# An attention and token/channel mixer kernel on one core: two key transposes and some sixty other steps change their places in a hand-written order

## The chip, the cores and the metric

The kernel runs on one NeuronCore of a Trainium2 chip. Its engines each work through a queue of their own, in order: TensorE (PE in the profile; its weight loads are PEld), VectorE (DVE), ScalarE (ACT), GpSimd (POOL) and SyncE (SP), which here only issues DMAs. The metric is the device time of one execution in microseconds.

## The reference

Eight batches, eight heads, 576 positions, head dimension 64. Keys and values are averaged over groups of eight positions (72 keys a head); the attention output of all heads forms x (576 x 512), which goes through a token mixer (576 to 256 to 576, with a residual) and a channel mixer (512 to 1536 to 512, with a residual).

```python
k_p = k.reshape(B, H, Sp, pool, D).mean(axis=3)
v_p = v.reshape(B, H, Sp, pool, D).mean(axis=3)
scores = scale * np.matmul(q, k_p.transpose(0, 1, 3, 2))
attn = softmax(scores)
x = np.matmul(attn, v_p)                        # heads side by side: (B, 576, 512)
h = np.maximum(xt @ w_tok1, 0.0) @ w_tok2       # xt: x with its two last axes exchanged
u = x + h.transpose(0, 2, 1)
out = u + np.maximum(u @ w_ch1, 0.0) @ w_ch2
```

## The kernel before

The work is cut into nine units (unit, L868). Units 0 to 7 run the channel mixer of 512 of the 576 rows of batch n; unit 8 runs the rows that are left of all batches. Between its matmuls, unit n carries the attention and token mixer of the next batches, so that TensorE always has something to do. The main work of a unit is a generator (unit_fast, L694) that yields 48 times, and after yield i the steps that PLAN[n] (L22) lists under i are issued: this is a *slot*. In units 0 to 5, slots 0 to 23 lie between halves of the twelve l1_tile (L557: four 512-column matmuls each, L560, then a ScalarE activation into GT, L564). The eight products that follow have twelve 256-column matmuls each (L699), yield after every four, and end with VectorE sums (L739, s and o). They form the second channel matmul with seven multiplications of blocks instead of eight, and so need sums of GT and of the weights, made by VectorE: "=1" (L603), "=2", "=3", "=4" (L588). In units 6 to 8 the first channel matmul is done in the same manner; the string under -1 in PLAN orders its steps (A1 to C7, L675), with L for a half tile and X for a third of the first product, and y0 to y3 and z0 to z3 make the sums that it needs (Y: on GpSimd).

A step "b.name" belongs to batch b. Those that matter here:

- lk, lq, lv: DMAs that load a batch's keys, queries, values, issued by GpSimd.
- K0, K1 (k0, V0, V1, v1 likewise): the average over eight positions of one half of the heads by three additions (pool8, L214: lines 217, 218 and 221 for keys, 223 for values), on GpSimd for capital letters and on VectorE for small ones. Both halves of the keys write the tile kp.
- kpT (L262): four TensorE transposes (L265) of kp and a ScalarE copy into kD. It needs both halves.
- Q0, Q1: VectorE transposes of the queries (L321). s0, s1, s2 (L326): scores, with the exponentials on ScalarE (L343); they need kD.
- av0 to av4 (L414): attention times values, then reciprocal and multiplication on VectorE (L426, L365) or, for aw, on ScalarE (L369).
- at0, at1 (L430): the first token matmul, five 512-column matmuls (L434) and a ScalarE activation into AT. u0 to u4 (L441): the second, and the residual on VectorE (L457).
- t0 to t3: transposes of u by TensorE (L465). Later batches do it by a write of u to HBM and a read in another shape (M0, M2, M4 and M, MT, on SP's queue), and a VectorE transpose of 32x32 blocks (T0 to T5, L499).
- g (gate, L864): VectorE sets a flag and GpSimd copies it (L866). What stands behind the copy on GpSimd therefore waits until VectorE has come so far; and VectorE's next setting of the flag waits until GpSimd has made the copy before.

Most TensorE steps write one of four PSUM banks, p1a to p1d. take (L82) hands out the bank that was given back first; a step that takes a bank waits on the chip until the engine that read it last is done. Scores and av steps use two other buffers ("p").

Of the kernel before, what the change touches and what calls it, by code (L numbers as in the profile page):

```python
# [20 lines left out]
HEAD = """LkA LkT LkB LvT Lq LvA LvB Lt1 Lk1 Lt2 Lc1b Lc1a Lq1 Lc1c Lv1 Lc1d p1 Lc2a Lc2b Lc2c d2 d2 d3 d1 d4 d4 c0 c1 prep q0 kp0 kp1 kt0 q1 d1 o0 kt1 kp2 e0 e1 q3 kt2 o1 q2 e3 vpool0 o3 e2 a00 vpool1 a02 o2 m01 d1 d1 m00 a04 X1 m03 a14 m02 X0 m04 p0 a10 a12 1.kpool m10 m14 m12 m13 m11 A1 A0 X2 X3 A2 A3"""  # L21
PLAN = [  # L22
# [9 lines left out]
]  # L32


# [906 lines left out]
```

## Time and profile before

| what | us |
|---|---|
| time, median of 3 runs | 260.82 (260.37 to 261.18) |
| the profiled execution, whole | 261.66 |
| its span, first to last instruction | 259.9 |
| TensorE busy in the span | 253.5 |
| VectorE / GpSimd / ScalarE busy | 206.7 / 149.5 / 128.7 |

The granted TensorE clock is 0.999 of full speed over the span. In a timeline row stand the start, the duration, engine, line, operation, the tiles (output<-inputs), shapes, and how many equal instructions the row merges; in brackets the engine's idle time before it and what ended it. TensorE's durations overlap, so that a matmul's price is read from the distance between starts.

### The profile page before, as it was taken

How to read it: one execution, taken by the hardware profiler on the slowest of the kernel's cores; microseconds unless marked ns; L12 is line 12 of the kernel's file. 1: busy time of each engine (PE TensorE's matmuls, PEld its weight loads, DVE VectorE, ACT ScalarE, POOL GpSimd, SP SyncE). 2: the span in 40 equal slices, each digit the busy share in tenths (PEclk: the TensorE clock that was granted, in tenths of full speed). 3: DMA queues.
4: the chain of work that ended last, by engine and by line, in shares of the span. 5: the costliest groups of instructions: out<-in, count | busy, mean ns of one | idle time of the engine just before them, and what ended most of it. 6: DMA issues, size and time to landing. Idle time of an engine off the chain costs nothing.

```text
span 259.9 us, 5596 instructions
## 1 busy us (share of the span) xinstructions
PE 253.5 (98%) x2211; PEld 169.3 (65%) x2211; DVE 206.7 (80%) x413; ACT 128.7 (50%) x242; POOL 149.5 (58%) x161
## 2 busy tenths in 40 slices
PE   8999999999989999999999999999999999999994
PEld 2785466764656644774478447844686678888883
DVE  5557569997768755898799586987999699999994
ACT  3354875049727565547652576056516631622720
POOL 8656226899989999678969983886211001411000
PEclk9999999999999999999999999999999999999999
DMA  7999999993074798569933883660225051702304
GB/s 142 194 201 206 205 207 209 206 230 91 3 117 65 120 226 160 167 102 226 247 93 53 192 215 83 91 162 2 103 62 156 9 159 45 203 3 49 115 3 161
DMA packets 31931, 34.32 MB, mean 132 GB/s; under 512 B 2976, under 2 KB 23968, under 8 KB 31904
## 3 DMA queue, kind: packets, MB, share of 16 engines
q0 software_dynamic: 17856, 17.64, 43.1%
q1 hardware_dynamic: 13632, 15.93, 20.1%
q10 hardware_dynamic: 416, 0.39, 0.5%
q8 instruction: 17, 0.28, 0.4%
q14 instruction: 10, 0.08, 0.1%
HBM read 38.99 MB, written 12.58 MB: 198 GB/s over the span
## 4 chain that ended last, share of the span: by engine, by line
PE 77%; DMA 13%; DVE 4%; POOL 2%; issue 2%; DVEq 0%; POOLq 0%
PE p1b L699 9%; PE p1c L699 8%; DMA w_ch<-in_moe_w_ch_dram 7%; PE p1c L560 6%; PE p1a L560 5%; PE p1d L560 5%; PE p1a L699 5%; PE p1b L560 5%; PE p1d L699 5%; DMA area<-in_moe_w_tok_dram 4%; PE p L334 3%; PE p L422 3%; DMA kr<-in_k_dram 3%; PE p1d L675 3%; PE p L675 2%; PE p1b L434 2%
## 5 line engine op out<-in xcount | busy, mean ns | idle before, releaser
L560 PEld LDWEIGHTS <-w_ch 128*128 128x128 bf16 x304 | 27.4, 98 | 29.6 <-issue 2.6
L699 PEld LDWEIGHTS <-area 128*128 128x128 bf16 x432 | 40.9, 98 | 8.0 <-issue 1.1
L866 POOL COPY flag<-flag 1x1 f32<-1x1 f32 x34 | 11.5, 339 | 58.6 <-DVE flag L865 58.6
L343 ACT ACTIVATE ex<-p 72x768 bf16<-72x768 f32 x42 | 31.6, 805 | 20.2 <-PE p L334 20.2
L699 PEld LDWEIGHTS <-GT 128*128 128x128 bf16 x312 | 29.6, 98 | 7.1 <-issue 2.3
L218 POOL TENSOR_TENSOR t<-t 72x512 f32<-72x512 f32 x21 | 30.2, 1437 | 1.6
L217 POOL TENSOR_TENSOR t<-kr 72x1024 f32<-72x1024 bf16 x11 | 23.4, 2123 | 0.4
L560 PE MATMUL p1c<-uT,w_ch 128*128 128x512 bf16 x84 | 22.9, 379 | 0.0
L217 POOL TENSOR_TENSOR t<-vr 72x1024 f32<-72x1024 bf16 x10 | 21.2, 2123 | 1.1 <-DMA vr<-in_v_dram 0.7
L560 PE MATMUL p1d<-uT,w_ch 128*128 128x512 bf16 x76 | 20.3, 379 | 0.0
L560 PE MATMUL p1a<-uT,w_ch 128*128 128x512 bf16 x72 | 20.0, 379 | 0.0
L365 DVE TENSOR_TENSOR x<-p,den 128x512 bf16<-128x512 f32 x27 | 18.7, 692 | 0.9
L560 PE MATMUL p1b<-uT,w_ch 128*128 128x512 bf16 x72 | 19.3, 379 | 0.0
L564 ACT ACTIVATE GT<-p1d 128x512 bf16<-128x512 f32 x19 | 11.5, 606 | 11.8 <-issue 7.5
L564 ACT ACTIVATE GT<-p1c 128x512 bf16<-128x512 f32 x21 | 12.7, 604 | 8.9 <-PE p1c L560 8.4
L422 PEld LDWEIGHTS <-ex 72*128 72x128 bf16 x280 | 13.0, 98 | 5.1 <-DVE xt L365 0.2
L699 PE MATMUL p1b<-area,area 128*128 128x256 bf16 x120 | 15.2, 273 | 0.0
L422 PE MATMUL p<-vp,ex 72*128 72x65 bf16 x280 | 14.3, 194 | 0.0
L564 ACT ACTIVATE GT<-p1b 128x512 bf16<-128x512 f32 x18 | 11.0, 611 | 5.1 <-PE p1b L560 5.0
L564 ACT ACTIVATE GT<-p1a 128x512 bf16<-128x512 f32 x18 | 10.9, 608 | 5.1 <-PE p1a L560 5.0
L457 DVE TENSOR_TENSOR u<-p1a,x 128x512 bf16<-128x512 f32 x10 | 7.3, 730 | 6.2 <-PE p1a L456 6.1
L221 POOL TENSOR_TENSOR kp<-t 72x256 bf16<-72x256 f32 x11 | 11.6, 1054 | 0.9
(259 smaller groups left out, 575.7 us busy)
## 6 DMA issues: line engine op xcount, KB each, us to landing
out_dram<-o SPq DMA_DIRECT2D x32, 256.0 KB, 3.9
qr<-in_q_dram POOLq DMA_DIRECT2D x7, 576.0 KB, 11.4
kr<-in_k_dram POOLq DMA_DIRECT2D x6, 512.0 KB, 9.8
vr<-in_v_dram POOLq DMA_DIRECT2D x6, 512.0 KB, 11.9
w_ch<-in_moe_w_ch_dram POOLq DMA_DIRECT2D x5, 512.0 KB, 16.5
mem<-u SPq DMA_DIRECT2D x10, 256.0 KB, 2.5
v<-mem SPq DMA_DIRECT2D x20, 128.0 KB, 2.9
area<-in_q_dram SPq DMA_DIRECT2D x2, 288.0 KB, 3.1
```

The lines of the kernel that those rows point to most:

```text
L217: eng.tensor_tensor(out=t4[:, 0:n], in0=t[:, hs, 0:4], in1=t[:, hs, 4:8], op=ALU.add)
L218: eng.tensor_tensor(out=t4[:, 0:n, 0:2], in0=t4[:, 0:n, 0:2], in1=t4[:, 0:n, 2:4], op=ALU.add)
L221: eng.tensor_tensor(out=dst.rearrange("j e l d -> j l e d"), in0=i0, in1=i1, op=ALU.add)
L334: nc.tensor.matmul(out=pss[l // 2][0:SP, l % 2, o:o + n1 - n0], lhsT=st["kD"][quad, g, db, :], rhs=st["qD"][quad, g, n0:n1, db], start=(db ...
L343: nc.scalar.activation(out=dst, in_=src, func=AF.Exp, scale=scale)
L365: nc.vector.tensor_tensor(out=dst, in0=view, in1=den[:, :, :, None].broadcast_to([n, a, 4, D]), op=ALU.mult)
L422: nc.tensor.matmul(out=ps[:, h // 4, (h % 4) * (D + 1):(h % 4 + 1) * (D + 1)], lhsT=st["ex"][:, h * S + n0:h * S + n0 + P], rhs=st["vp"][: ...
L560: nc.tensor.matmul(out=ps, lhsT=w_ch1[:, kk, m * P:(m + 1) * P], rhs=uT[kk], start=(kk == 0), stop=(kk == 3))
L564: nc.scalar.activation(out=GT[:, :, m, :], in_=ps.rearrange("p (h n) -> p h n", h=2), func=AF.Relu)
L675: nc.tensor.matmul(out=ps[:, j], lhsT=a(2 * g + j, kk), rhs=c(kk), start=k in (1, 2, 5) and j == 0 and kk == 0, stop=kk == 1, skip_group_c ...
L699: nc.tensor.matmul(out=ps[i] if split else ps[:, i], lhsT=chunk(u, i, a(m)), rhs=w(m), start=start and m == 0 and (i == 0 or split), stop= ...
L866: nc.gpsimd.tensor_copy(out=flag[:, 1:2], in_=flag[:, 0:1])
```

## The change

Only PLAN is changed: no step's code, no tile and no load. In unit 1, 2.kpT goes from slot 2 to slot 0, 2.s0 from 4 to 3, and 3.kpT from slot 29 to slot 26, ahead of 2.at1. In unit 3 a gate is added in slot 2, ahead of 5.K1. In units 2 to 8 steps move by mostly one to four slots, a few further, and the orders of the fast steps of units 6, 7 and 8 are altered. Its core, unit by unit, with the moved entries alone (first the line of before, then that of after):

```diff
 unit 1
-    2: "2.kpT", 4: "2.s0", ... 26: "2.at1", ... 28: "2.at0 =4 g", 29: "3.kpT"
+    0: "2.kpT", 3: "2.s0", ... 26: "3.kpT 2.at1", ... 28: "2.at0 =4 g"
 unit 2
-    6: "3.av3 3.av4", 13: "6.lk", 14: "=3 3.at0", 20: "3.u0 3.u3", 21: "3.u2", 24: "3.M0 3.M2", 31: "4.s1 3.MT 3.T3 3.T0"
+    5: "3.av4", 6: "3.av3", 12: "g 6.lk 3.at1", 13: "3.at0", 16: "=3", 20: "3.u0 3.u2 3.u3", 22: "3.M0", 24: "3.M2", 30: "3.M 3.T3"
 unit 3
-    1: "4.av0", 2: "5.K1", 8: "4.at1", 9: "5.k0 4.at0", 12: "5.V0", 15: "4.u3 5.kpT 5.V1", 17: "5.s0", 22: "4.M2 4.u0"
-    25: "3.T4 =1 3.T5", 28: "g 4.M0", 29: "4.M", 30: "5.s2", 35: "5.aw2", 40: "4.T0 5.av3 5.av4", 43: "4.T2 5.at0 5.at1"
+    2: "4.av0 g 5.K1", 6: "5.V0", 7: "4.at1", 8: "5.k0", 9: "4.at0", 13: "5.Q0 4.u1 3.T5", 16: "5.kpT", 18: "=3 5.Q1 4.u0"
+    19: "5.s0", 21: "3.T4", 25: "4.M2 =1", 28: "=4 4.M0 5.s2", 29: "g", 30: "4.M", 36: "5.aw2", 37: "4.T2 5.av1", 38: "4.T0"
 unit 4
-    8: "7.Q1 5.u0 7.lk", 9: "5.u2 5.u3", 15: "6.s0 5.M2 g", 16: "6.V0", 20: "5.M", 21: "g", 22: "=3 6.Q1", 24: "6.s1", 28: "=2"
+    2: "6.K0 5.u2", 9: "5.u0 5.u3", 11: "5.u1 7.lk 6.kpT", 14: "g 5.M2 g", 17: "6.V0 6.Q1", 21: "5.M", 23: "=3", 25: "=2 6.s1"
 unit 5
-    3: "z0", 5: "6.av4", 12: "6.at0 6.at1", 17: "6.u3 6.u1 7.s0", 19: "7.V0", 23: "z1", 24: "z2 =1", 31: "6.M2", 40: "6.y0 z3", 42: "7.s2"
+    4: "6.av4", 6: "z0", 10: "6.at0", 12: "z2", 15: "6.at1 7.v1", 17: "7.V0 g 6.u1", 19: "6.u3", 21: "z1 7.s0", 25: "6.M0 6.M2", 38: "z3", 39: "7.s2"
 unit 7
-    -1: "B1 A1 A2 C1 B2 C2 A6 B6 A5 B5 A7 C6 B7 C5 A3 B3 ...", 0: "g 7.Y2", 26: "=2", 43: "8.y2"
+    -1: "A1 A2 B1 C1 C2 B2 A6 B6 A5 A7 B5 B7 A3 C6 C5 B3 ...", 7: "7.Y2 7.Y3", 23: "=2 g"
 unit 8
-    -1: "A1 A2 B1 B2 A6 C1 B6 A5 ...", 0: "8.y3", 22: "=1 =2"
+    -1: "A1 B1 A2 A6 C1 B2 B6 A5 ...", 0: "8.y3", 4: "8.y2", 22: "=1", 24: "=2"
```

In the built programs every engine has the same instructions as before, but for one flag setting on VectorE and its copy on GpSimd; SP's queue keeps its order.

16 rows, old and new, of the table PLAN are left out of this document.

## The prediction

> **What bounds the kernel now.** I read the page first, then the busy time by stretches, then TensorE's waits, and last the timelines of the engines where TensorE's matmuls start later than their own spacing allows.
>
> ```profile
> span 259.9 us, 5596 instructions
> PE 253.5 (98%) x2211; PEld 169.3 (65%) x2211; DVE 206.7 (80%) x413; ACT 128.7 (50%) x242; POOL 149.5 (58%) x161
> ...
> 52.00:78.00 26.00, 25.29 (x235) 14.83 (x233) 19.83 (x33) 15.85 (x34) 24.05 (x21) 1.00 0.57 110
> ```
>
> TensorE (PE) is busy for 253.5 of 259.9 us. A new order removes no matmul, so it can only win or lose idle time, and in the middle of the kernel the stretch from 52 to 78 us shows 0.71 us of it: the end of unit 0 and unit 1, where the key transposes stand. This is that place on TensorE.
>
> ```profile
> 70.77 1.03 PE L434 MATMUL p1b<-x,w_tok 128*128 128x512 bf16 x4
> ...
> 71.85 1.04 PE L699 MATMUL p1a<-w_ch,GT 128*128 128x256 bf16 x8
> 72.72 1.03 PE L434 MATMUL p1d<-x,w_tok 128*128 128x512 bf16 x4
> ...
> 73.80 0.60 PE L699 MATMUL p1a<-w_ch,GT 128*128 128x256 bf16 x4
> 74.24 0.29 PE L265 MATMUL p1b<-ident,kp 72*128 72x72 bf16 x4
> 74.65 1.03 PE L699 MATMUL p1d<-area,area 128*128 128x256 bf16 x8
> 76.28 0.59 PE L456 MATMUL p1a<-AT,w_tok 128*128 128x512 bf16 x2 [0.60 <-DVE o L739]
> ```
>
> A row's duration runs past the next start, so I use distances between starts. Eight 256-column matmuls take 0.87 (71.85 to 72.72), five 512-column ones of step at 1.08 (70.77 to 71.85, its fifth matmul among them). The eight from 74.65 are through at 75.52, but u3 starts at 76.28: 0.76 us lost. Four matmuls (L265) are priced at 0.13, by the starts of the second fence below, so TensorE was free at 74.37 and lost 0.28 before 74.65. These two, 1.04 us together, are the largest waits from there to the end.
>
> ```profile
> 69.90 0.69 DVE L365 TENSOR_TENSOR x<-p,den 128x512 bf16<-128x512 f32 x1
> 70.51 0.95 DVE L603 TENSOR_TENSOR area<-GT 128x1536 bf16<-128x1536 bf16 x1
> 73.07 0.69 DVE L739 TENSOR_TENSOR s<-p1c,u 128x512 f32<-128x512 f32 x1 [1.61 <-issue]
> ...
> 75.54 0.69 DVE L739 TENSOR_TENSOR o<-p1a,s 128x512 f32<-128x512 f32 x1
> ```
> ```profile
> 74.00 0.60 ACT L436 ACTIVATE AT<-p1d 128x512 bf16<-128x512 f32 x1 [1.36 <-PE p1d L434]
> ```
> ```profile
> 56.02 0.85 POOL L221 TENSOR_TENSOR kp<-t 72x256 bf16<-72x256 f32 x1
> ...
> 66.25 0.84 POOL L221 TENSOR_TENSOR kp<-t 72x256 bf16<-72x256 f32 x1
> ...
> 69.36 1.26 POOL L218 TENSOR_TENSOR t<-t 72x512 f32<-72x512 f32 x1
> 70.70 1.45 POOL L221 TENSOR_TENSOR kp<-t 72x256 bf16<-72x256 f32 x1
> ...
> 72.86 0.17 POOL L866 COPY flag<-flag 1x1 f32<-1x1 f32 x1
> ```
>
> Both waits are for PSUM banks. The third fast product (74.65) takes p1d, which ScalarE reads until 74.60. Step u3 takes p1a, which VectorE's o releases at 75.54+0.69 = 76.23, and TensorE starts 0.05 later. That o is late because VectorE stood for 1.61 us in front of 73.07: the gate of slot 25 waits until GpSimd has run the flag copy of slot 18, at 72.86, and GpSimd was busy with unit 3's keys.
>
> **Unit 1, the first moved transpose.** 2.kpT now stands after two matmuls of the unit instead of four.
>
> ```profile
> 55.95 1.03 PE L560 MATMUL p1d<-uT,w_ch 128*128 128x512 bf16 x4
> 56.81 0.59 PE L560 MATMUL p1b<-uT,w_ch 128*128 128x512 bf16 x2
> 57.24 0.29 PE L265 MATMUL p1c<-ident,kp 72*128 72x72 bf16 x4
> 57.37 0.60 PE L560 MATMUL p1b<-uT,w_ch 128*128 128x512 bf16 x2
> ```
>
> Four matmuls take 0.86, two 0.43, so TensorE arrives at 56.38. Its keys are ready at 56.02+0.85 = 56.87, usable at 56.92: a new wait of 0.54 us. Behind it on TensorE stand all the unit's matmuls, and through them VectorE and ScalarE; GpSimd is not behind it, since its row of work goes on from its own queue. This matters next.
>
> **Unit 1, the second.** 3.kpT moves ahead of 2.at1, which began at 70.77; with the 0.54, TensorE is there at 71.31. When are the keys ready? In the trace L221 ends at 72.15, but it took 1.45 us where the same pass took 0.84 or 0.85: it started at 70.70, while VectorE's L603 (from 70.51) was running, and ended 0.69 after that one's end. The reverse order stands in unit 2:
>
> ```profile
> 103.81 1.96 DVE L603 TENSOR_TENSOR area<-GT 128x1536 bf16<-128x1536 bf16 x1
> ```
> ```profile
> 102.83 2.12 POOL L217 TENSOR_TENSOR t<-vr 72x1024 f32<-72x1024 bf16 x1
> 105.03 1.87 POOL L218 TENSOR_TENSOR t<-t 72x512 f32<-72x512 f32 x1
> ```
>
> There GpSimd's L217, already running, was not slowed (2.12); L603 waited for its end at 104.95 and ended 0.82 later; the next L218 waited for that. The one that starts first runs undisturbed. Here L603 follows the x of 69.90, which TensorE paces, so the 0.54 moves it from 70.51 to 71.05, after L221's start at 70.70. GpSimd goes first: keys at 70.70+0.84 = 71.54, usable at 71.59, a wait of 0.28. If VectorE kept the right of way, they would come at 72.15 as before, usable at 72.20. I take 71.59, by the rows of unit 2, and keep 72.20 for the range.
>
> The Trainium skill says the same of who goes first (SBUF — State Buffer, section "Who interferes with whom": whichever of the two issues first has the shared port pair for the whole instruction). It speaks against the move only if the order of issue stays as it was; by it the keys come at 71.54, and without it at 72.15.
>
> From 3.kpT to u3 the starts give 0.13 + 1.08 (at1) + 0.87 + 1.08 (at0) + 0.44 (73.80 to 74.24) + 0.87 = 4.47, so u3 starts at 76.06, against 76.28: **0.22 gained** at this point. The two bank waits are gone in that sum for this reason: banks are given out first in, first out, and one more take and release ahead of at1 shifts the cycle. The third product now takes at1's bank, and u3 takes at0's, whose copy follows at0's end by 0.80 (73.80 to 74.60): at0 ends at 74.75, the copy at 75.55, 0.51 before u3. VectorE's o no longer holds u3. So the new waits of 0.54 and 0.28 buy 1.04; and the first is free, since without it TensorE would only wait longer at the second.
>
> **Unit 3, the added gate.** Its flag copy stands ahead of 5.K1 on GpSimd; its memset stands behind 4.av0 on VectorE and itself waits for the preceding copy only, done by 115.5.
>
> ```profile
> 116.74 2.13 POOL L217 TENSOR_TENSOR t<-kr 72x1024 f32<-72x1024 bf16 x1
> 118.95 2.15 POOL L218 TENSOR_TENSOR t<-t 72x512 f32<-72x512 f32 x1
> 121.18 1.17 POOL L221 TENSOR_TENSOR kp<-t 72x256 bf16<-72x256 f32 x1
> ```
> ```profile
> 116.81 0.69 DVE L365 TENSOR_TENSOR x<-p,den 128x512 bf16<-128x512 f32 x1
> ...
> 118.77 1.21 DVE L217 TENSOR_TENSOR t<-kr 72x1024 f32<-72x1024 bf16 x1
> 120.02 1.64 DVE L218 TENSOR_TENSOR t<-t 72x512 f32<-72x512 f32 x1
> 121.69 0.95 DVE L221 TENSOR_TENSOR kp<-t 72x256 bf16<-72x256 f32 x1
> ...
> 124.49 0.69 DVE L457 TENSOR_TENSOR u<-p1b,x 128x512 bf16<-128x512 f32 x1
> ```
> ```profile
> 125.49 0.29 PE L265 MATMUL p1a<-ident,kp 72*128 72x72 bf16 x4
> ```
>
> 5.K1 starts at about 117.7 instead of 116.74. Its three passes alternate with VectorE's 5.k0, each waiting for the other as above: taken apart, GpSimd works 2.13, 1.13, 0.69 and VectorE 1.11, 0.56, 0.29, and in turn they end at 119.8, 120.9, 122.0, 122.6, 123.3, 123.6. So 5.k0 ends at 123.6, not 122.64, and u2, Q0 and u1 behind it follow at the 0.61 of such passes (69.90 to 70.51 above); u1 starts at about 124.8 and releases its bank at 125.5. 5.kpT, one slot later than before, needs this bank at 125.49+0.43 = 125.92. **Cost 0**, covered by 0.4 us. If the cover fails because all three of 5.k0's passes wait for a whole GpSimd pass (2.13+1.27+0.84 on its own 1.96), it ends at 124.97, u1 at 127.0, and TensorE waits 1.1. I take 0 and keep 1.1.
>
> **The other moves.** Engine by engine, many change nothing: unit 2's =3 and 6.lk, unit 4's 7.lk and 5.M, unit 7's Y2 only change the slot, and stand between the same neighbours on their queues; memory-queue order (SP's) is the same throughout. Of those that do change an order, u0, u2, av0, av4, at0, at1 and s0 to s2 keep their operands ahead of TensorE when the distances of the traced steps are laid out in the new order (5.s1 is the tightest, by 0.14), and T0, T2, T5, z2 and unit 4's =2 leave crowded stretches of VectorE for idle ones. Cost 0; they could win back what is left of TensorE's small gaps:
>
> ```profile
> 111.69 0.71 PE L699 MATMUL p1b<-w_ch,area 128*128 128x256 bf16 x5
> ...
> 254.86 1.36 PE L814 MATMUL p<-area,GT 128*128 128x256 bf16 x11
> ```
>
> These are the first and the last of eleven after 78 us; start distances less the form's own spacing give 0.88 together, 0.15 each for these two. I take nothing of it. In unit 7, C2 goes ahead of B2:
>
> ```profile
> 222.86 0.68 DVE L659 TENSOR_TENSOR GT<-p1a,ex 128x512 bf16<-128x512 f32 x1
> ...
> 223.27 0.60 PE L675 MATMUL p1b<-qr,kr 128*128 128x256 bf16 x4
> ```
>
> B2's sum on VectorE then takes about the place that C2's has here (to 223.7), and B5, which reuses B2's bank, comes a step later than 223.27, at 223.71. Cost 0.05, at most 0.2.
>
> **Sum.** -0.22 (unit 1) + 0 (unit 3) + 0.05 (unit 7) = -0.17 us. On the profiled execution that makes a span of 259.7 instead of 259.9; its whole time was 261.66, 0.84 above the median of 260.82 of the runs shown, and I carry the difference over: **260.6 us**.
>
> **The rivals.**
> - *Relief pays* (faster): VectorE, freed of half a dozen transposes and sums in crowded places, also ends the ten gaps ahead of the last, 0.74 in all: 259.9. For it: nearly all of them end on VectorE or ScalarE. Against: most are chains of a matmul and its own copy, which no queue order shortens.
> - *Keys as late as before* (slower): VectorE's L603 still takes the turn from GpSimd's L221, keys usable at 72.20, u3 at 76.67, which is 0.39 after 76.28: 261.2. For it: the margin in issue order is only 0.35 us. Against: unit 2's rows.
> - *The gate in unit 3* (slower): it decides as soon as u1 ends after 125.87, and costs up to 1.1: 261.7.
> - *Nothing moves*: the bank cycle does not shift where it counts and the waits only change names: 260.8.
>
> **How the numbers follow.** Forecast 0.48 (260.2 to 261.0), relief 0.20, late keys 0.12, the gate 0.15, nothing 0.05. About 0.3% (0.78 us) is what a measurement of this kernel can tell from no change: under 260.04 is faster, over 261.60 slower. Relief and 0.02 of the forecast's tail are faster, 0.22; the gate and 0.01 are slower, 0.16; the rest, 0.62, is the same. The range runs from 259.8 to 261.7, from relief to the gate's full price.
>
> **What would show it.** Right: in the new profile the matmuls of the first moved transpose start near 56.92 and those of the second near 71.6, GpSimd's L221 before the latter takes about 0.85, VectorE's L603 beside it about 1.3, u3 follows the third product's eight matmuls without a gap, and o is not what it waits for. Wrong: that L221 at 1.45 again, u3 after 76.5, a gap before the L265 group near 125.9, or VectorE waiting at the new memset.

## The result, and the profile after

| | before | after |
|---|---|---|
| median of six executions each, us | 260.71 (260.29 to 261.18) | 262.28 (262.11 to 262.43) |
| ratio after / before | | 1.0062, 95% interval 1.0051 to 1.0073 |
| the profiled execution, whole / span | 261.66 / 259.9 | 262.24 / 260.4 |

The changed kernel is 1.57 us slower. Its profiled execution is like its median; that of before was 0.95 above its own median, so the two traces differ by 0.5 in span where the medians differ by 1.57. The page and the middle stretch after:

```profile
span 260.4 us, 5598 instructions
PE 252.9 (97%) x2211; PEld 169.5 (65%) x2211; DVE 207.4 (80%) x414; ACT 129.3 (50%) x242; POOL 148.5 (57%) x162
...
52.00:78.00 26.00, 25.91 (x240) 14.96 (x239) 20.65 (x35) 17.08 (x35) 24.02 (x22) 1.00 0.64 124
```

The 0.71 of idle time of this stretch is down to 0.09. The timelines of TensorE, GpSimd and VectorE there:

```profile
55.68 0.59 PE L560 MATMUL p1d<-uT,w_ch 128*128 128x512 bf16 x2
56.11 0.29 PE L265 MATMUL p1b<-ident,kp 72*128 72x72 bf16 x4
...
70.71 0.30 PE L265 MATMUL p1c<-ident,kp 72*128 72x72 bf16 x4
...
74.32 1.04 PE L699 MATMUL p1a<-area,area 128*128 128x256 bf16 x8
75.19 0.59 PE L456 MATMUL p1c<-AT,w_tok 128*128 128x512 bf16 x2
```
```profile
55.14 0.84 POOL L221 TENSOR_TENSOR kp<-t 72x256 bf16<-72x256 f32 x1
...
69.81 0.84 POOL L221 TENSOR_TENSOR kp<-t 72x256 bf16<-72x256 f32 x1
```
```profile
70.25 1.22 DVE L603 TENSOR_TENSOR area<-GT 128x1536 bf16<-128x1536 bf16 x1
```

Both PSUM waits are gone, the banks are those that the prediction named, and u3 follows the eight matmuls at their own distance (74.32 to 75.19). L221 goes ahead of L603 and takes 0.84, L603 1.22. But the first transpose did not wait: its keys were there at 55.98, 0.13 before TensorE, not at 56.87. GpSimd was 0.9 earlier than in the trace of before, and TensorE 0.3. Further on, TensorE shows two waits that the trace of before does not have, and in unit 3 none ahead of 5.kpT:

```profile
124.90 0.29 PE L265 MATMUL p1c<-ident,kp 72*128 72x72 bf16 x4
...
168.30 1.02 PE L560 MATMUL p1c<-uT,w_ch 128*128 128x512 bf16 x4 [0.61 <-DVE uT L499]
...
224.19 0.60 PE L675 MATMUL p1a<-qr,kr 128*128 128x256 bf16 x4 [0.68 <-DVE GT L659]
```

The first is the start of unit 5 (5:m0), behind VectorE's 5.T2; the second is B5 of unit 7, behind B2's sum. By start distances they cost 0.68 and 0.84 to 0.85. What stands behind each, on VectorE and GpSimd in unit 7, and on VectorE in unit 4:

```profile
221.59 0.69 DVE L659 TENSOR_TENSOR GT<-p1c,ex 128x512 bf16<-128x512 f32 x1
222.32 1.22 DVE L665 TENSOR_SCALAR GT<-GT 128x512 bf16<-128x512 bf16 x1
223.46 0.68 DVE L659 TENSOR_TENSOR GT<-p1a,ex 128x512 bf16<-128x512 f32 x1
```
```profile
222.24 1.15 POOL L588 TENSOR_TENSOR qr<-uT,qr 128x512 bf16<-128x512 bf16 x1
```
```profile
160.91 0.45 DVE L499 STREAM_TRANSPOSE uT<-v 128x256 uint32<-128x256 uint32 x1 [0.74 <-DMA v<-mem]
```

C2's relu (L665), which the new order puts ahead of B2's sum, starts 0.08 after GpSimd's 7.Y3 and ends 0.15 after it. In unit 4, 5.T1 stands 0.74 for the last piece of 5.M. The DMA view of 138 to 163 us gives, from issue to landing, the loads of unit 7's keys (here and below, unit n's keys are those of batch n) and the writes that 5.M reads back (x2: the middle of two):

```profile
kr<-in_k_dram POOLq DMA_DIRECT2D x1, 512.0 KB, 9.6
mem<-u SPq DMA_DIRECT2D x2, 256.0 KB, 5.1
```

The same rows in the trace of before:

```profile
kr<-in_k_dram POOLq DMA_DIRECT2D x1, 512.0 KB, 8.1
mem<-u SPq DMA_DIRECT2D x2, 256.0 KB, 2.5
```

### The profile page after: what moved, and what is told of

Its sections match the earlier page's. It is cut to its first block, busy times and chain, and to the rows that moved or that the text cites. A ratio compares the mean times of both kernels' runs of the same rounds, so it can differ in the third digit from the quotient of the medians.

```text
span 260.4 us, 5598 instructions
## 1 busy us (share of the span) xinstructions
PE 252.9 (97%) x2211; PEld 169.5 (65%) x2211; DVE 207.4 (80%) x414; ACT 129.3 (50%) x242; POOL 148.5 (57%) x162
## 4 chain that ended last, share of the span: by engine, by line
PE 72%; DVE 12%; DMA 8%; issue 3%; ACT 3%; SPq 1%; POOL 0%; DVEq 0%; ACTq 0%; POOLq 0%
PE p1c L560 6%; PE p1b L560 6%; PE p1a L699 6%; PE p1a L560 6%; PE p1d L699 5%; PE p1d L560 5%; PE p1c L699 4%; PE p1b L699 4%; DMA mem<-u 3%; DVE s L739 3%; PE p L422 3%; DMA v<-mem 2%; PE p1d L675 2%; PE p L334 2%; DMA kr<-in_k_dram 2%
## 5 line engine op out<-in xcount | busy, mean ns | idle before, releaser
L866 POOL COPY flag<-flag 1x1 f32<-1x1 f32 x35 | 10.7, 305 | 60.6 <-DVE flag L865 60.6
L217 POOL TENSOR_TENSOR t<-kr 72x1024 f32<-72x1024 bf16 x11 | 24.0, 2178 | 0.3
L564 ACT ACTIVATE GT<-p1c 128x512 bf16<-128x512 f32 x22 | 13.3, 605 | 16.5 <-PE p1c L560 8.2
L560 PE MATMUL p1a<-uT,w_ch 128*128 128x512 bf16 x76 | 21.1, 380 | 0.0
L560 PE MATMUL p1b<-uT,w_ch 128*128 128x512 bf16 x76 | 20.2, 379 | 0.0
L560 PE MATMUL p1d<-uT,w_ch 128*128 128x512 bf16 x64 | 18.0, 379 | 0.0
L699 PE MATMUL p1a<-area,area 128*128 128x256 bf16 x120 | 15.6, 273 | 0.0
L603 DVE TENSOR_TENSOR area<-GT 128x1536 bf16<-128x1536 bf16 x9 | 10.6, 1183 | 4.7 <-ACT GT L564 4.7
L564 ACT ACTIVATE GT<-p1a 128x512 bf16<-128x512 f32 x19 | 11.5, 606 | 4.5 <-PE p1a L560 4.3
L369 ACT ACTIVATE x<-p,den 128x64 bf16<-128x64 f32 x40 | 8.8, 337 | 7.6 <-DVE den L426 7.6
L655 ACT COPY ex<-p 128x512 f32<-128x512 f32 x6 | 3.5, 590 | 17.7 <-PE p L675 17.7
## 6 DMA issues: line engine op xcount, KB each, us to landing
vr<-in_v_dram POOLq DMA_DIRECT2D x6, 512.0 KB, 11.9
```

The costliest lines, as they stand in the source:

```text
L217: eng.tensor_tensor(out=t4[:, 0:n], in0=t[:, hs, 0:4], in1=t[:, hs, 4:8], op=ALU.add)
L369: nc.scalar.mul(dst[:, a, h], view[:, a, h], den[:, a, h:h + 1])
L560: nc.tensor.matmul(out=ps, lhsT=w_ch1[:, kk, m * P:(m + 1) * P], rhs=uT[kk], start=(kk == 0), stop=(kk == 3))
L564: nc.scalar.activation(out=GT[:, :, m, :], in_=ps.rearrange("p (h n) -> p h n", h=2), func=AF.Relu)
L603: eng.tensor_tensor(out=S[0], in0=g[1][0], in1=g[1][1], op=ALU.add)
L699: nc.tensor.matmul(out=ps[i] if split else ps[:, i], lhsT=chunk(u, i, a(m)), rhs=w(m), start=start and m == 0 and (i == 0 or split), stop= ...
```

## The experiments

Seventeen runs. e1 to e4, e5 to e8, e9 to e12, e13 to e15 and e16 with e17 each shared a chip, five in all, with the kernel before beside them; the ratio is to that, an estimate of its own with its interval and not the quotient of the two medians.

| run | median us | before us | ratio (95% interval) |
|---|---|---|---|
| e1 before again | 260.69 | 260.82 | 0.9995 (0.9971 to 1.0019) |
| e2 unit 7's order back | 260.70 | 260.82 | 0.9996 (0.9976 to 1.0015) |
| e3 unit 4 back | 261.41 | 260.82 | 1.0024 (1.0002 to 1.0045) |
| e4 unit 1 alone | 260.69 | 260.82 | 0.9984 (0.9963 to 1.0005) |
| e5 after again | 261.84 | 260.95 | 1.0043 (1.0028 to 1.0059) |
| e6 unit 7's order alone | 261.31 | 260.95 | 1.0024 (1.0006 to 1.0042) |
| e7 7.Y3 later | 260.59 | 260.95 | 0.9992 (0.9972 to 1.0011) |
| e8 unit 4 alone | 261.00 | 260.95 | 1.0012 (0.9993 to 1.0031) |
| e9 unit 1, 5.av4 later | 261.37 | 261.06 | 1.0011 (0.9993 to 1.0028) |
| e10 late write | 260.85 | 261.06 | 0.9986 (0.9969 to 1.0004) |
| e11 late keys, before | 261.79 | 261.06 | 1.0034 (1.0016 to 1.0053) |
| e12 late keys, unit 1 | 261.46 | 261.06 | 1.0015 (0.9996 to 1.0035) |
| e13 write last | 262.16 | 260.75 | 1.0061 (1.0041 to 1.0082) |
| e14 write last, 5.T1 later | 261.15 | 260.75 | 1.0011 (0.9989 to 1.0032) |
| e15 after, third time | 262.09 | 260.75 | 1.0051 (1.0031 to 1.0071) |
| e16 mended | 260.74 | 261.13 | 0.9996 (0.9974 to 1.0018) |
| e17 unit 1 alone again | 260.81 | 261.13 | 0.9988 (0.9970 to 1.0006) |

**Which trace of before is the usual one (e1, e11, e12).** e1 is the kernel before, unchanged. e11 and e12 do the last addition of 2.K0 twice on GpSimd (e12 with unit 1's line of the changed kernel); its result stays the same.

```diff
-    pool8(..., t == "k")
+    pool8(..., t == "k", 2 if (b, t, g) == (2, "k", 0) else 1)
...
-    eng.tensor_tensor(out=dst.rearrange("j e l d -> j l e d"), ...)
+    for _ in range(again): eng.tensor_tensor(out=dst.rearrange("j e l d -> j l e d"), ...)
```

> The kernel before once more, for a second trace. The first trace's execution took 261.66, 0.95 more than the median of 260.71. Theory: about 0.4 of that is in the head, where the first trace's matmuls came up to their full rate at 6.66 us and the changed kernel's at 5.33, and the rest in single waits of the first trace; the second trace then has a span near 259.0 and shows TensorE earlier by about 0.4 at the end of the head. Rival: the second trace stands step by step where the first stood, span 259.9, and the excess is an accident of the one whole time.

> The kernel before with the last addition of 2.K0 done twice on GpSimd, so that GpSimd runs 0.92 us later from there on, as it did (0.87 to 0.89) in the first trace of before. Theory: that lateness alone makes the wait of 0.76 in front of u3: =3's gate comes late, VectorE's o with it, and the time is 0.7 above the kernel before in its usual execution, 261.4 to 261.6; the trace shows u3 over 0.6 late. Rival: u3's wait in the first trace came of the head (its late start), and the added 0.92 is absorbed: 260.8 to 261.0.

> The same doubled addition of 2.K0, with unit 1's line of the changed kernel. This is the ground on which the forecast was worked out. The forecast's sum: 2.kpT waits 0.5 for the keys, 3.kpT waits 0.2 to 0.3, u3 does not wait: 0.22 under the run with the doubled addition and the old line. Rival 1: the first transpose's wait is not paid for by the second, both bank waits go, and the gain is 0.6 to 0.8. Rival 2: keys of unit 3 as late as VectorE's L603 makes them, 3.kpT waits 0.9, and the time is 0.3 or more above the run with the old line.

The second trace of before has a span of 258.6, 1.2 less than the first; 0.2 of that is in the head (what stands ahead of unit 0), not the 0.4 of the theory. Its TensorE timeline at the place of the old waits:

```profile
74.40 1.03 PE L699 MATMUL p1d<-area,area 128*128 128x256 bf16 x8
75.28 0.59 PE L456 MATMUL p1a<-AT,w_tok 128*128 128x512 bf16 x2
```

There is no wait at u3: 74.40 to 75.28 is the eight matmuls. GpSimd shows why, first in the second trace, then in the first:

```profile
50.08 0.84 POOL L221 TENSOR_TENSOR kp<-t 72x256 bf16<-72x256 f32 x1
...
55.16 0.85 POOL L221 TENSOR_TENSOR kp<-t 72x256 bf16<-72x256 f32 x1
```
```profile
50.73 1.66 POOL L221 TENSOR_TENSOR kp<-t 72x256 bf16<-72x256 f32 x1
```

In the first trace GpSimd came 0.65 later to this pass, which then took 0.82 more; the last pass of the keys came 0.86 later (56.02 to 55.16), the gate 1.5 later, and so VectorE's o held u3. Up to this pass all the kernels are the same program, so that all 19 traces tell how usual that is: the pass took 1.66 to 1.68 in three (the first of before, e8, e16) and 0.84 to 0.85 in sixteen. In e11 the same lateness, brought about by the added pass, brings the wait back; e12 is the same with the new line:

```profile
55.54 1.03 PE L560 MATMUL p1d<-uT,w_ch 128*128 128x512 bf16 x4
...
76.13 0.59 PE L456 MATMUL p1a<-AT,w_tok 128*128 128x512 bf16 x2 [0.85 <-DVE o L739]
```
```profile
55.32 0.59 PE L560 MATMUL p1d<-uT,w_ch 128*128 128x512 bf16 x2
56.59 0.30 PE L265 MATMUL p1b<-ident,kp 72*128 72x72 bf16 x4 [0.67 <-POOL kp L221]
...
74.84 1.04 PE L699 MATMUL p1a<-area,area 128*128 128x256 bf16 x8
75.72 0.59 PE L456 MATMUL p1c<-AT,w_tok 128*128 128x512 bf16 x2
```

From the unit's first matmul to u3 it is 76.13-55.54 = 20.59 with the old line and 75.72-55.32 = 20.40 with the new: 0.19 gained, with a wait at 2.kpT and none at u3. That is the forecast's ground and, but for 0.03, its sum; the medians of e11 and e12 differ by 0.33. On the usual ground it is 75.28-55.70 = 19.58 in e1 (unit start 55.70) and 75.19-55.68 = 19.51 after: 0.07 gained. e8, with the old unit 1, had u3's wait of itself (20.34), e6 had not (19.57).

**Unit 1 alone (e4, e17), and one step more (e9).** e4 and e17 take unit 1's line of PLAN alone; e9 also moves 5.av4, in unit 3:

```diff
-    40: "4.T0 5.av3 5.av4"
+    40: "4.T0 5.av3", 41: "5.av4"
```

> The kernel before with unit 1's line of the changed kernel alone. Theory: unit 1 gains what the trace of the changed kernel shows to its end, about 0.7, and nothing behind it gives it back: 260.0. Rival 1, the forecast's working: 0.22, so 260.5. Rival 2: the gain is given back further on, since units 2 to 7 wait for loads and VectorE and not for TensorE: 260.7 or more.

> The kernel before with unit 1's line alone, beside the mended kernel. Its first measurement was 0.9984 [0.9963, 1.0005] of before. Theory: the same again, 0.2 to 0.4 under the kernel before, as far from it as the mended kernel. Rival: nothing, within 0.1; then the first was chance.

> The kernel before with unit 1's line of the changed kernel, and 5.av4 one slot later in unit 3. Theory: unit 1's 0.25 is given back at 138.62, where 5.av4 waits 0.285 (0.08 in the kernel before) for ScalarE's last row of 5.aw2, whose chain starts at VectorE's =1 beside GpSimd and does not come earlier with TensorE; with a product's four matmuls (0.44) ahead of it 5.av4 does not wait, and the 0.2 is kept: 260.4 to 260.5, against 260.8 to 260.95 for the kernel before in the same call. Rival: the work that comes behind 5.av4 (5.at0, 5.at1) waits for it instead, and the time is that of unit 1 alone (0.1 to 0.2 under before) or more.

In e4 TensorE runs 0.25 ahead of e1 from unit 1's end (0.19 of it from the head, which differs from one execution to the next) to 138, and 0.05 ahead from there on. VectorE's =1 of unit 3 in e4, then in e1, and the GpSimd pass beside each:

```profile
129.53 1.52 DVE L603 TENSOR_TENSOR area<-GT 128x1536 bf16<-128x1536 bf16 x1
```
```profile
129.78 1.32 DVE L603 TENSOR_TENSOR area<-GT 128x1536 bf16<-128x1536 bf16 x1
```
```profile
128.97 1.26 POOL L218 TENSOR_TENSOR t<-t 72x512 f32<-72x512 f32 x1
```
```profile
129.00 1.27 POOL L218 TENSOR_TENSOR t<-t 72x512 f32<-72x512 f32 x1
```

L603 ends 0.82 to 0.83 after GpSimd's pass in both, however early it is issued, and GpSimd does not follow TensorE. From there the lateness seems to go by VectorE's queue to 5.aw2 and to 5.av4, which no run shows by itself. Moving 5.av4 only moved the wait: in e9 TensorE stood for 5.av4's product in 5.at0, and the 0.2 was not kept. Its median is 0.31 over before, with no change inside the interval.

```profile
141.33 0.38 PE L434 MATMUL p1a<-xt,w_tok 128*128 128x512 bf16 x1 [0.41 <-DVE xt L365]
```

The theory of e4, 260.0, failed: 260.69. The two measurements of unit 1 alone, 0.9984 and 0.9988, lie on the gain's side, and no change (1) is in both intervals.

**Unit 7 (e2, e6, e7).** e2 is after with the old order of fast steps in unit 7, e6 before with the new one. e7 keeps the new order, puts 7.Y2 four slots earlier and adds a gate, so that 7.Y3 starts behind B2's relu:

```diff
-    0: "g", 7: "7.Y2 7.Y3"
+    0: "g", 3: "7.Y2", 5: "g 7.Y3"
```

> The changed kernel with unit 7's order of fast steps as before, all else changed. Theory: C2 ahead of B2 puts C2's relu on VectorE beside GpSimd's 7.Y3, which makes it 1.22 us instead of 0.5, B2's sum comes late and B5 waits 0.84; with the old order that goes, and the time is 261.45 (0.83 under 262.28). Rival: 7.Y3, which also moved in slots, delays VectorE whatever the order, and the wait only changes its place: 262.1 to 262.3.

> The kernel before with unit 7's order of fast steps of the changed kernel alone. Theory: C2's relu meets GpSimd's 7.Y3 here too, since nothing else of the change bears on unit 7: the relu takes 1.2, B5 waits 0.8 to 0.9, and the time is 261.6. Rival: the collision needs the slots of the changed kernel as well (7.Y2 and 7.Y3 together in slot 7), and the time stays at 260.8.

> The changed kernel with one more gate, which lets GpSimd start 7.Y3 only when VectorE is through B2's relu; the order of the fast steps stays that of the changed kernel. Theory: the shared work of C2's relu and 7.Y3 is all that costs: the relu takes 0.4 to 0.55, B2's sum comes at about 222.7 instead of 223.46 on the changed kernel's clock, B5 waits under 0.15, 7.Y3 ends near 225 and A4 (226) does not wait; 0.7 to 0.8 less than the changed kernel of the same call. Rival: it is the order itself (B2's sum behind C2's sum and relu on VectorE); then B5 still waits 0.5 or more.

In e6 the relu on VectorE and B5 on TensorE:

```profile
222.04 1.22 DVE L665 TENSOR_SCALAR GT<-GT 128x512 bf16<-128x512 bf16 x1
```
```profile
223.91 0.60 PE L675 MATMUL p1a<-qr,kr 128*128 128x256 bf16 x4 [0.68 <-DVE GT L659]
```

In e7 the same relu, 7.Y3 behind it on GpSimd, and B5:

```profile
221.75 0.29 DVE L665 TENSOR_SCALAR GT<-GT 128x512 bf16<-128x512 bf16 x1
```
```profile
223.33 1.15 POOL L588 TENSOR_TENSOR qr<-uT,qr 128x512 bf16<-128x512 bf16 x1
```
```profile
222.33 0.60 PE L675 MATMUL p<-qr,vr 128*128 128x256 bf16 x4
222.77 0.60 PE L675 MATMUL p1a<-qr,kr 128*128 128x256 bf16 x4
```

0.29 instead of 1.22, and B5 at its distance of 0.44. By start distances, B5 lost 0.84 to 0.87 in the traces of after, e3, e5, e6 and e15, and nothing in e2 and in the five with 7.Y3 later (e7, e10, e13, e14, e16). It is the collision and not the order: e7 has the order. e7 is 1.25 under after on the same chip (e5), of which 0.86 is this by e5's trace; the other 0.39 is not accounted for. e2, at 260.70, is 0.75 under its theory, since its trace has no wait at 5:m0 either. e6's median is only 0.36 above before; its interval, 0.06 to 0.42%, which is 0.16 to 1.1 us, holds the 0.84 that its trace shows.

**Unit 4 (e3, e8, e10, e13, e14, e5, e15).** e3 is after with the old line of unit 4, e8 before with the new one, e5 and e15 after unchanged. e10, e13 and e14 have e7's gate; e10 and e13 delay 5.u3 and 5.M2, e14 is e13 with 5.T1 behind =4:

```diff
 e10
-    9: "5.u0 5.u3", 14: "g 5.M2 g", 15: "6.s0", 17: "6.V0 6.Q1"
+    9: "5.u0", 14: "g g", 15: "6.s0 5.u3", 17: "5.M2 6.V0 6.Q1"
 e13
+    9: "5.u0", 14: "g g", 15: "6.s0", 17: "6.V0 6.Q1", 19: "5.u3", 20: "5.M2"
 e14, beside e13
-    29: "6.s2 5.T1 g", 30: "=4"
+    29: "6.s2 g", 30: "=4 5.T1"
```

> The changed kernel with unit 4's line as before, all else changed. Theory: unit 4's new places make the writes of u to memory go out 1 us earlier, in the middle of the loads of unit 7's keys, where they take 5.1 us instead of 2.5; 5.M and the transposes 5.T follow late, and 5:m0 waits 0.61; with the old line the writes take about 2.5 again and the time is 261.6 (0.7 under 262.28). Rival: the early writes come of unit 1's gain, which brings everything forward against the loads, not of unit 4's line; then the writes still take about 5 and the time stays at 262.2.

> The kernel before with unit 4's line of the changed kernel alone. Theory: it makes unit 7's keys and with them the writes of 5.M0 and 5.M2 land late (9 us for the keys instead of 7.4, 4 to 5 for the writes instead of 2.0 to 2.8), which leaves 5.T1 a margin of 0.2 or less: 260.8 to 261.5, with 5.M's last piece behind 159.5. Rival: the late keys in two of six traces are an accident of the run; then 7.4 and 2.3 here, and 260.8.

> The changed kernel once more, beside the others and beside the kernel before. What is known: with unit 7's order undone it took 260.70, with unit 4's line undone 261.41, and the kernel before 260.82. Theory: unit 7's order costs about 0.85 in every execution, and the wait at 5:m0 (0.6 in the first trace of the changed kernel, none in the trace with unit 7's order undone, although unit 4's line stood there too) comes when 5.M's last piece lands after VectorE has reached 5.T1; so the time is 261.6 where that piece lands before 160.0, and 262.3 where it lands near 160.9. Rival: the wait at 5:m0 belongs to the changed kernel in every execution, and the trace without it was an exception: 262.3 whatever the landing.

> The changed kernel with the gate that puts 7.Y3 later (it took 260.59), and in unit 4 5.u3 six slots and 5.M2 three slots later, so that the write of 5.M2 goes out some 2.5 us later. Theory: 5.M's last piece then lands near 161, VectorE stands 0.8 to 1.2 in front of 5.T1, its queue behind it is full to the unit's end, and 5:m0 waits for 5.T2 by that less 0.2, as in the first trace of the changed kernel: 0.6 to 1.0, and 261.2 to 261.6. Rival: VectorE makes the stall good before 5.T2, 5:m0 waits under 0.2, and the time stays at 260.6 to 260.8; then the wait of the first trace had another cause.

> The changed kernel with the gate that puts 7.Y3 later, and in unit 4 5.u3 at slot 19 and 5.M2 at slot 20, so that the write of 5.M2 goes out near 154.5, behind the loads. Theory: the write takes 2.0, 5.M goes out at 156.6 and its last piece lands near 161; VectorE comes to 5.T1 at 159.3 to 159.9 and stands 1.1 to 1.6 there; its queue is full from there to 5.T2, so 5:m0 waits for 5.T2 by that less 0.2 to 0.5: 0.7 to 1.3, and 261.4 to 261.9 where 260.6 to 260.85 would stand without. Rival: VectorE makes it good before 5.T2; 5:m0 waits under 0.2, and the time is 260.6 to 260.9.

> The same with 5.T1 behind =4 on VectorE. Theory: =4 (0.95) runs while the last piece is still under way, so that VectorE loses 0.2 to 0.7 at 5.T1 instead of 1.1 to 1.6, and 5:m0 waits 0.9 less: 0 to 0.4, and 0.6 to 0.9 less time than with 5.T1 ahead of =4. Rival: the wait at 5:m0 does not hang on what VectorE loses at 5.T1 (for instance on 5.T2's own piece); then it is as long as with 5.T1 ahead of =4.

> The changed kernel a third time, for one more pair of landing and wait as the runs give them. Theory: where 5.M's last piece lands before VectorE comes to 5.T1 (159.9 on the first trace's clock), 5:m0 waits under 0.1 and the time is 0.85 to 0.95 above the kernel before, all of it unit 7's order; where it lands near 160.9, 5:m0 waits 0.6 and the time is 1.5 above. Rival: a wait at 5:m0 with a landing before 159.5, or none with one behind 160.8.

e3 took 0.87 less than the first measurement of after, but on another chip, where after itself was not run. e8 shows neither late keys (7.3) nor late writes (2.1 and 2.3), and no wait at 5:m0: unit 4's line alone does not make them. e5 and e15 show after without the wait at 5:m0 in the trace; in e15 the last piece landed at 159.90 and 5.T1 came at 160.24. So the wait comes in some executions of after and not in others. The six of the first measurement, within 0.3 of each other, fit the one with it; the medians of e5 and e15, 0.89 and 1.34 over before, fit none and a mixture, but only the profiled executions show it. e10 missed its aim: 5.M2's write, issued 2.9 after 5.M0's, landed only 0.9 behind it, and nothing waited. The DMA view of e10, at the issue of the one and then of the other:

```profile
mem<-u SPq DMA_DIRECT2D x1, 256.0 KB, 4.0
```
```profile
mem<-u SPq DMA_DIRECT2D x1, 256.0 KB, 2.0
```

A write beside the loads takes up to 5.1 (after, above) and one that goes out as they end, or behind them, 2.0, so that a late write costs little. In all 19 traces 5.M0's write lands 0.2 to 1.0 behind the last piece of unit 7's keys, 2.0 to 4.9 after its issue. This suggests that late keys make 5.M late and so take 5.T1's margin; no run moved the keys alone. In e13 the write was late enough. 5.T1 on VectorE and 5:m0 on TensorE, of e13 and then of e14:

```profile
161.63 0.45 DVE L499 STREAM_TRANSPOSE uT<-v 128x256 uint32<-128x256 uint32 x1 [1.57 <-DMA v<-mem]
```
```profile
169.02 0.81 PE L560 MATMUL p1c<-uT,w_ch 128*128 128x512 bf16 x3 [0.80 <-DVE uT L499]
```
```profile
161.23 0.45 DVE L499 STREAM_TRANSPOSE uT<-v 128x256 uint32<-128x256 uint32 x1 [0.60 <-DMA v<-mem]
```
```profile
167.71 1.02 PE L560 MATMUL p1c<-uT,w_ch 128*128 128x512 bf16 x4 [0.43 <-DVE uT L499]
```

What VectorE loses at 5.T1 TensorE loses too, but for 0.06 to 0.10, at the unit's end: 1.57 and 1.51 in e13 (with an av step ahead of 5:m0), 0.60 and 0.50 in e14, 0.74 and 0.68 in the first trace of after. The two times differ by 1.01, as the two stalls do (0.97); both waits are 0.1 to 0.2 longer than the theories had them.

Part of the late landing is a move of unit 3. Its gate, in slot 28 before, stands in slot 29 after, and there VectorE sets the flag behind a product's o instead of ahead of it. The flag copy on GpSimd and, behind it on the same queue, the issue of unit 7's keys, in e1 and then in after:

```profile
134.03 0.18 POOL L866 COPY flag<-flag 1x1 f32<-1x1 f32 x1 [2.35 <-DVE flag L865]
...
144.09 1.28 POOL L131 DMA_DIRECT2D kr<-in_k_dram  x2
```
```profile
134.90 0.17 POOL L866 COPY flag<-flag 1x1 f32<-1x1 f32 x1 [2.62 <-DVE flag L865]
...
144.99 1.29 POOL L131 DMA_DIRECT2D kr<-in_k_dram  x2
```

Both come 0.87 to 0.90 later, of which TensorE's own lateness in after is 0.26 (table below). Measured from the start of TensorE's first fast product in unit 4 (156.87 in the first trace of before), the keys go out 10.9 ahead in all ten traces with the new line of unit 3 (e3 among them) and 11.5 to 11.9 ahead in the nine with the old one, while 5.T1, where it does not wait, comes 4.2 behind in the traces of both sides that have it ahead of =4. So the change starts the keys' load 0.6 later in every trace, against a margin of 1.9 to 2.1; no run moves this gate alone. What stays open is why the keys take 7.1 to 8.1 in some traces (both of before, e3 to e6, e8, e11, e12, e16, e17) and 8.3 to 9.7 in others (the first of after, e2, e7, e9, e10, e13 to e15). The long ones are, but for e9, of kernels with the new line of unit 3.

**Both losses taken away (e16).** It is e7 with 5.T1 behind =4.

> The changed kernel with both causes mended: the gate that puts 7.Y3 behind B2's relu, and 5.T1 behind =4 on VectorE, with the write of 5.M2 where the changed kernel has it. Theory: what is left of the change is unit 1, which takes 0.2 to 0.3 off on the mean and, where GpSimd runs late, the whole wait at u3: 0.2 to 0.4 under the kernel before of the same call, and no execution more than 1.2 over the fastest. Rival: the rest of the moves (unit 2's gate near 110.5, the end of unit 3) takes it back: within 0.1 of the kernel before.

260.74 against 261.13, but a ratio of 0.9996 with no change well inside: the rival (nothing left of the gain) cannot be told from the theory. Its executions spread over 2.3, not the 1.2 of the theory. Its trace has neither wait. The medians of e4, e7, e10, e16 and e17 are 0.1 to 0.4 under before, none by more than its interval, and e1, with no change at all, is 0.13 under.

## Why the prediction was wrong

TensorE's starts in four traces, less the start of the same matmul in the second trace of before (e1), at places behind which all have the same order:

| place (start in e1) | first trace of before | after | e5, after again | e7 |
|---|---|---|---|---|
| unit 0 begins (23.97) | +0.20 | -0.17 | +0.23 | +0.05 |
| behind unit 1's waits (76.70) | +1.01 | -0.08 | +0.16 | -0.01 |
| unit 3 (118.90) | +1.19 | +0.17 | +0.44 | +0.26 |
| unit 4 (147.15) | +1.25 | +0.26 | +0.53 | +0.35 |
| unit 5 (170.52) | +1.25 | +0.90 | +0.51 | +0.33 |
| unit 6 (200.34) | +1.25 | +0.89 | +0.50 | +0.32 |
| unit 8 (239.05) | +1.25 | +1.74 | +1.37 | +0.33 |
| last product (253.61) | +1.25 | +1.81 | +1.44 | +0.40 |

Read down: after loses 0.25 between unit 1 and unit 3, 0.09 in unit 3, 0.64 at the end of unit 4, 0.85 in unit 7; its gain of 0.07 in unit 1 against the usual execution is too small to be seen here.

The sum said 0.17 less, and 1.57 more was measured: 1.74 apart. Of that, 0.80 is unit 7 (0.85 for 0.05), 0.68 the wait at 5:m0 (for 0) and 0.15 unit 1 (0.07 for 0.22); the 0.11 that is left is less than the executions differ.

- **The base.** The step that failed first, though not the dearest, is "its whole time was 261.66, 0.84 above the median of 260.82 of the runs shown, and I carry the difference over". The excess was not a constant: of the 1.25 by which the first trace ended behind e1's, 0.76 was the very wait at u3 that was to be gained. With GpSimd late as in that trace the sum is right (0.19 for 0.22, e11 and e12); with GpSimd as usual the gain is 0.07.
- **Unit 1, the mechanisms.** The keys of unit 3 at GpSimd's undisturbed 0.84, L603 at about 1.3, the shifted banks and u3 without o: all as worked out. The wait of 0.54 at 2.kpT was as much an accident as the one it was to buy out: where GpSimd was late it came (0.60 in e16, 0.67 in e12), else not. The forecast's 0.28 at 3.kpT measured 0.20 (70.71, by start distances). Late keys of unit 3, the rival, did not come.
- **Unit 3's gates.** Cost 0 holds for the added one: 5.kpT starts at 124.90 without a gap. The working holds too: less the 1.0 by which the first trace of before ran behind after there, the six passes of 5.K1 and 5.k0 end within 0.1 of the times worked out (118.83 to 122.57). The rival at 261.7 had another mechanism than the loss that came. The other gate of unit 3, which moved from slot 28 to 29, was not worked out at all; it sends out unit 7's keys 0.6 later.
- **Unit 7.** "Cost 0.05, at most 0.2" is the term that was mis-sized: 0.85. The step counted C2's and B2's sums, as if they changed places alone. C2's relu goes with its sum, from GT to GT, and meets GpSimd's 7.Y3. Unit 2's rows had shown that the one that starts first runs undisturbed; the prediction used that for L221 and did not look for a pass of GpSimd at the new place. In the first trace of before it met 7.Y3 as well (0.53, ended 0.15 behind it), but TensorE did not have to wait for what stood behind it. The Trainium skill (SBUF — State Buffer, section "Who interferes with whom") names tensor_scalar, which L665 is, among the operations that can take the shared pair; the traces agree, with 1.22 beside 7.Y3 in after and 0.29 alone in e7.
- **Units 2 to 6.** "Cost 0" left out 5.M's reads: 5.T1 comes 1.9 and 2.1 behind the landing in the traces of before, and in the three of after 1.3, 0.3 or, in the first, only when the piece has landed. It is the landing that came late, and not 5.T1 early. The prediction laid out TensorE's and VectorE's queues and the order of SP's, but not the landings. The wait at 5:m0 costs 0.68 where it comes. The 0.25 is mostly a wait behind VectorE near 110.5 (0.22); e6 and e11 have one there too (0.36 and 0.55) without unit 2's moves, so that it cannot be put down to the change.

The range, 259.8 to 261.7, was made from single mishaps; before's 260.7 and unit 7's 0.85 alone make 261.6, and no rival had either place where it happened.

## What to carry to other kernels

When the profiled execution is slower than the median, look for the excess among its waits before pricing a gain there: another trace, or an added delay, tells a lasting wait from an accident. When an operation changes places, carry every instruction that it issues to the new place, and see what GpSimd does there. A read that waits for a write and a load has a margin as well; when the loads come late, the margin goes without any order on their own queue having changed. And a gate that moves by one slot moves all that stands behind it on the other engine: here a load that went out ten us further on.

## What the runs showed of the hardware

A VectorE relu of 128x512 bf16 in SBUF took 0.29 with GpSimd idle (e7), and ended 0.15 after GpSimd's pass, at 1.22, when that had started 0.08 earlier (after). A write of 256 KB from SBUF took 2.0 behind two loads (512 and 64 KB; e13, e14), and 4.0 to 4.9 where the first of the two writes went out over 3 us before the loads had landed (after, e2, e7, e10, e13 to e15). Executions of the kernel before on one chip (that of e1) lay between 259.94 and 262.82, a spread of 2.9, at a granted TensorE clock of 0.997 to 1.000. The Trainium skill (DMA: Bandwidth & Descriptors, section "Latency and other measured facts") puts an HBM access at 0.2 us on average and 2 us at high load. A write of 256 KB goes out in many packets (in e13's DMA views of 150 to 152 and 154 to 156 us each is under 8 KB), so that the 2.0 to 2.9 more that it took beside the loads is not the same quantity, and no run here shows the time of one access.
